# A spectral mixing layer and an MLP on one core: the sum of two loaded pieces made by an accumulating DMA instead of by VectorE

## The chip, the cores and the metric

The kernel runs on one core of one Trainium2 chip. The time is that of one execution on the device in microseconds, taken as the median of several runs. Beside it stands one execution recorded by the hardware profiler, whose span reaches from the first to the last instruction.

## What is computed

The input x has 2048 rows of 640 numbers, in float32. The reference normalizes each row, and adds three things: x itself, an MLP of the normalized rows with a GELU between two dense layers (640 to 1536 to 640), and a Fourier mixing of the normalized rows, of which only the real part is kept:

```python
xn = _layernorm(x)
a = einsum("bsd,ed->bse", xn, dft_hid_re)
b = einsum("bsd,ed->bse", xn, dft_hid_im)
y = einsum("ts,bse->bte", dft_seq_re, a) - einsum("ts,bse->bte", dft_seq_im, b)
out = x + y + gelu(xn @ w1 + b1) @ w2 + b2
```

Here `dft_seq_re` and `dft_seq_im` are 2048 x 2048 matrices that are inputs like any other; the kernel calls them cr and ci. The change lies in the stage that multiplies with these two (the sequence transform).

## The kernel before, in words

**Precision.** Every float32 operand of a product is kept as two parts of type float32r: ScalarE copies the high part (`high`, L186), VectorE subtracts it from the operand to get the low part (`low`, L189), and a product is three matmuls, high by high, high by low and low by high (`product`, L300 to L302). The two parts of a moving operand of the sequence transform lie in the tile `as`, which has three places that are used in turn.

**Blocks and pieces.** After the normalization, the MLP and the preparation of the stationary operands (the first 330 us) the sequence transform runs over 8 blocks (h, t): h is a half of the work along the sequence, t one of four groups of 512 rows of cr and ci. The order is h = 0 with t = 0 to 3, then h = 1 with t = 3, 0, 1, 2; after the sixth and the eighth block comes a stage that multiplies with the hidden-dimension matrices (`hidden_beside`, `hidden_entry`). For each block four raw pieces are loaded from DRAM: cr1, cr2, ci1 and ci2, the two halves of the columns of cr and of ci. A piece is 1 MB, and `steps_of_load` brings it in four DMAs of 256 KB, one for each quadrant of 32 partitions, in runs of 512 bytes, all issued by SyncE (L503). The pieces lie in the places `raw_a`, `raw_b` and, in the first half only, `raw_c`. `turn` (L520) then transposes a piece in 32 x 32 blocks on VectorE, in two halves u = 0, 1 (L524), out of `raw` into the tile where it is held: `r` for cr1 and cr2, `rt` for ci1 and ci2. When the second half of a piece has been transposed, its place is free, and `turn` issues the load of the piece that takes it next (`heir`). Two pieces of the last block are an exception: their loads are put off into the hidden stage before it (`put_off`, L1616 and L1618).

**Seven products.** A block takes seven products instead of eight, in the manner of Strassen, which need sums of the pieces. VectorE makes them in place on the held tiles, each in two halves: f5 puts ci1 + ci2 on ci1 (L563), f6 adds that to cr1, f3 adds the new cr1 to cr2, and f7 subtracts ci2 from cr1; all go through `add` (L463). The products use, in this order, cr1, cr2, ci1 (the sum), cr1 after f6, cr2 after f3, cr1 after f7, and ci2. ci1 as loaded is used for nothing but f5.

**The order of the work.** It is written out by hand, and every engine runs its own instructions in that order. A block is 14 entries (seven products by two halves u) of 18 matmuls each in the first three products and 12 in the others, with 12 more in entry 12. Entry n does its matmuls, then the steps in `pre`, then `form(n + 3)`, which makes the two parts for the third entry after it, then the steps in `post`. `beside` (L1328) gives `pre` and `post`: in the first block the transposition of ci2 and f5, f6, f3, f7; in the others f6, f3 and f7 of the block itself, the transpositions of the next block's pieces (ci1 beside entries 2 and 3), the sums that collect the results, and their loads and stores. f5 for a later block stands behind the last entry of the block before (L1436, L1473) or beside the first entries of the hidden stage (L1589, L1590). In the first block the transposition of ci1 comes ahead of the loop: behind it VectorE makes the last stationary operands (`build`, part "c") and then the low part for entry 3.

**Queues.** SyncE issues nearly all DMAs. GpSimd issues the stores of intermediate results in the first 266 us and a few stores of the output at the end.

Of the kernel before, what the change touches and what calls it, by code (L numbers as in the profile page):

```python
# [13 lines left out]
ALU = mybir.AluOpType  # L14

P = 128
Q = 4
B = 32
# [8 lines left out]
def kernel(  # L27
# [45 lines left out]
    nc = tc.nc  # L73
# [388 lines left out]
    def add(dst, a, b, op=ALU.add):  # L462
        nc.vector.tensor_tensor(dst, a, b, op=op)  # L463
# [28 lines left out]
    def steps_of_load(g):  # L492
        if g is None:
            return []
        h, t, kind = pieces[g]
        m, half = KINDS[kind]
        r = A["raw3"] if home[g] == "c" else A["raw"]
        raw[g] = r.tile([P, NB, NK * B], F32, tag=f"raw_{home[g]}", bufs=1, name=f"raw{g}")
        v = rows_of((cr, ci)[m], t)

        def quadrant(q):
            s0 = q * SQ + (half * NS // 2 + h * NK) * B
            nc.sync.dma_start(raw[g][q * B : (q + 1) * B], v[:, :, s0 : s0 + NK * B])  # L503

        return [lambda q=q: quadrant(q) for q in range(Q)]

    def held(kind, u):

        return {
            "cr1": lambda: A["r01"][:, 0, u],  # L510
            "cr2": lambda: A["r01"][:, 1, u],
            "ci1": lambda: A["rt2"][:, 0, u],
            "ci2": lambda: A["rt2"][:, 1, u],
        }[kind]()
# [32 lines left out]
    def form(n):  # L547
# [7 lines left out]
        else:  # L555
# [3 lines left out]
                split(a[:, 0], a[:, 1], src)  # L559
            else:  # L560
                split(a[:, 0, 0], a[:, 1, 0], src)

    def f5(u):  # L563
        add(held("ci1", u), held("ci1", u), held("ci2", u))

    def f6(u):
        add(held("cr1", u), held("cr1", u), held("ci1", u))
# [760 lines left out]
    def beside(h, t, n):  # L1328
# [14 lines left out]
        def g(k, acc, first=False, op=ALU.add):  # L1343
            return lambda: gather(h, t, k, acc, first, op)
# [18 lines left out]
        if b == 0:  # L1363
            T = lambda k, u: (lambda: turn(piece[0, 0, k], u))
            pre = {
                11: [g("v2", x_)],
            }.get(n, [])
            post = {
                0: [T("ci2", 0), F(f5, 0)],
                1: [g("u1", x_, True), T("ci2", 1), F(f5, 1), F(f6, 0), F(f6, 1)],  # L1370
                2: [lambda: load_xo(NT - 1)],
                3: [F(f3, 0), g("u", us, True)],
                4: [F(f3, 1), g("u1", y_)],
                5: [g("v2", z_, True), F(f7, 0)],
                6: [F(f7, 1)],
                7: [g("u2", x_, True), nturn("ci1", 0)],
                8: [nturn("ci1", 1)],
                9: [nturn("cr1", 0)],
                10: [g("u2", z_)],
                11: [nturn("cr1", 1)],  # L1380
                12: [nturn("cr2", 0)],
                13: [nturn("cr2", 1), nturn("ci2", 0), nturn("ci2", 1)],
            }.get(n, [])
        else:
            pre = {
                0: [F(f3, 0)] if ahead else [F(f6, 0)],
                1: [F(f3, 1)] if ahead else [F(f3, 0)],
                2: [nturn("ci1", 0)],
                3: [nturn("ci1", 1)],
                4: [F(f7, 0)],  # L1390
                5: [F(f7, 1)],
                6: [nturn("cr2", 0)],
                7: [nturn("cr2", 1)],
                8: [nturn("cr1", 0)],
                9: [nturn("cr1", 1)],
                10: [g("u2", z_)],
                11: [g("v2", x_)],
                12: [nturn("ci2", 1)] if direct else [nturn("ci2", 0)],
            }.get(n, [])
            post = {  # L1400
                0: [] if ahead else [F(f6, 1)],
                1: [g("u1", x_, True)] + ([] if ahead else [F(f3, 1)]),
                3: [g("u1", y_), g("u", us, True)],
                4: [t1(0)] if second else [],
                5: [g("v2", z_, True)],
                6: [t1(2)] if second else [],
                7: [g("u2", x_, True)],
                11: [nturn("ci2", 0)] if direct else [],
                12: [] if direct else [nturn("ci2", 1)],
                13: [t1(1)] if second else [],  # L1410
            }.get(n, [])
        if h == 0:
# [19 lines left out]
                }.get(n, [])  # L1432
            elif n == 13:
                post.append(lambda: later.append(lambda: put(h, t, "v", "v1")))
            if n == 13:
                post += [lambda: f5(0), lambda: f5(1)]  # L1436
        else:
            if p == 0 and n in (9, 10):
                post.append(lambda: load_part(blocks[b + 1][1], ("u1", "u")[n - 9]))
# [30 lines left out]
            if n == 13 and p == 1:  # L1470
                post += [lambda: open_g(b), lambda: [load_g(b, i) for i in range(3, len(A["g", b]))]]
            if n == 13 and direct:
                post += [g("v", vs, op=ALU.subtract), g("v1", x_), lambda: f5(0), lambda: f5(1)]  # L1473
        return pre, post


# [33 lines left out]
    def hidden_beside(b, n):  # L1510
# [64 lines left out]
        def last_columns():  # L1575
# [3 lines left out]

        yb1, yb2 = in_two(0), in_two(1)  # L1580
        yb4 = to(yo[tb, 4], vs, f"yb4_{tb}", lambda: store(tb, yo[tb, 4], 4 * B, DQ, *((nc.gpsimd,) if last else ())))
        f5s = [lambda u=u: f5(u) for u in range(2)] if not last else [lambda: None] * 2
        f6s = [lambda u=u: f6(u) for u in range(2)] if not last else [lambda: None] * 2
        v1 = lambda: add(s(1, "v1"), s(1, "v1"), x_)
        end = lambda: add(bank(X + 1), bank(X + 1), A["end"])
        pre = [v1] if n == 17 and not last else []
        post = {

            0: [lambda: gather(1, tb, "v1", z_), lambda: gather(1, tb, "v", vs, op=ALU.subtract), f5s[0]],  # L1589
            1: [f5s[1]],  # L1590
            3: [to(ya[:, :, : 2 * B], x_, f"ya1_{ta}")],
            2: [last_columns] if last else [],
            4: [t2(0)],
# [163 lines left out]
```

## Time and profile before

| | |
|---|---|
| median of 3 runs | 852.09 us (851.99 to 852.13) |
| profiled execution: span | 849.9 us |
| median of the runs less that span (what lies around it) | 2.2 us |
| instructions | 10599 |
| TensorE, VectorE, ScalarE, GpSimd busy | 841.9, 686.7, 368.6, 67.7 us |
| DMA moved | 166.53 MB, 196 GB/s on the mean |
| sequence transform with the hidden stages, first to last matmul | 330.30 to 844.57 us |

The profile names the engines PE (TensorE's matmuls), PEld (its loading of weights), DVE (VectorE), ACT (ScalarE), POOL (GpSimd) and SP (SyncE); a "q" behind a name marks the engine's own sequencer, which issues DMAs. L503 is line 503 of the kernel. `rt<-raw` means that tile rt is written from tile raw. A row of the groups gives line, engine, operation, tiles and shapes, the count behind "x", then busy time in us, the mean ns of one, the idle time before them and what ended it. A row of the timeline gives start and length in us, the engine, the line, the operation, the tiles, and in brackets how long the engine had been idle and what released it. A row of one line or tile gives the shortest, median and longest duration in ns and the first and last start in us, and for DMAs a line with the shortest, median and longest time from issue to landing. A row of the windows gives the stretch, its length, each engine's busy time and instructions in the order PE, PEld, DVE, ACT, POOL, then TensorE's granted clock, the share of the 16 DMA engines and GB/s. A row of the waits gives who waited for whom, the total in us, how often, and the longest.

### The profile page before, as it was taken

The numbers are of one execution on the slowest core, as the hardware profiler recorded it, in microseconds if no ns is written. First come the engines' busy times: TensorE is split into PE (matmuls) and PEld (weight loads), VectorE is DVE, ScalarE is ACT, GpSimd is POOL, SyncE is SP. The second block draws the span as 40 slices with busy tenths as digits, with TensorE's granted clock in tenths as the row PEclk, the third lists the DMA queues.
The fourth block names the chain that finished last, engine by engine and source line by source line (L and its number), as shares of the span: only waits on it lengthen the run. The fifth ranks groups of instructions, "written<-read, shape, count | busy, mean of one in ns | idle before, by whom it ended". The sixth has DMA issues, their size and how long they took to land.

```text
span 849.9 us, 10599 instructions
## 1 busy us (share of the span) xinstructions
PE 841.9 (99%) x3711; PEld 696.7 (82%) x3711; DVE 686.7 (81%) x909; ACT 368.6 (43%) x527; POOL 67.7 (8%) x116
## 2 busy tenths in 40 slices
PE   8999999999999999999999999999999999999997
PEld 7888888888888888888888888888888888888886
DVE  7979889767844778979978887889967998885687
ACT  7655666654453555443444344232323433323241
POOL 0440024222301000000000000000000000000002
PEclk9999999999999999999999999999999999999999
DMA  8995667878977897958744679763745799705464
GB/s 230 288 248 158 139 163 250 260 223 305 262 192 199 333 323 138 209 120 193 158 137 107 167 220 283 165 144 99 214 150 156 229 237 234 303 19 180 124 172 108
DMA packets 199141, 166.53 MB, mean 196 GB/s; under 512 B 61648, under 2 KB 170192, under 8 KB 198576
## 3 DMA queue, kind: packets, MB, share of 16 engines
q1 hardware_dynamic: 188320, 140.42, 62.7%
q0 software_dynamic: 7600, 24.91, 8.7%
q10 hardware_dynamic: 3168, 0.52, 0.3%
q8 instruction: 29, 0.48, 0.2%
q14 instruction: 24, 0.20, 0.1%
HBM read 115.75 MB, written 46.14 MB: 190 GB/s over the span
## 4 chain that ended last, share of the span: by engine, by line
PE 98%; DMA 1%; DVE 0%; ACT 0%; SPq 0%; issue 0%; ACTq 0%
PE banks L301 29%; PE banks L302 29%; PE banks L300 29%; PE banks L320 10%; DMA row<-in_A_x_dram 1%; PE banks L682 0%; DVE st L215 0%; ACT xp L714 0%; SPq L208 0%; DVE yo L1722 0%; DVE mv L216 0%; ACT mv L707 0%; DVE mv L708 0%; ACTq L707 0%
## 5 line engine op out<-in xcount | busy, mean ns | idle before, releaser
L186 ACT ACTIVATE as<-r 128x1024 fp32r<-128x1024 f32 x80 | 85.0, 1062 | 171.1 <-PE banks L302 150.4
L300 PE MATMUL banks<-as,xab 128*128 128x512 f32 x407 | 158.3, 389 | 0.0
L302 PE MATMUL banks<-as,xab 128*128 128x512 f32 x407 | 158.3, 389 | 0.0
L301 PE MATMUL banks<-as,xab 128*128 128x512 f32 x407 | 158.3, 389 | 0.0
L189 DVE TENSOR_TENSOR as<-r,as 128x1024 fp32r<-128x1024 f32 x80 | 97.2, 1215 | 38.1 <-ACT as L186 38.0
L301 PEld LDWEIGHTS banks<-as,xab 128*128 128x128 f32 x407 | 76.4, 188 | 15.9
L302 PEld LDWEIGHTS banks<-as,xab 128*128 128x128 f32 x407 | 76.4, 188 | 15.8
L300 PEld LDWEIGHTS banks<-as,xab 128*128 128x128 f32 x407 | 76.4, 188 | 15.8
L300 PE MATMUL banks<-as,xc 128*128 128x512 f32 x224 | 87.1, 389 | 0.0
L301 PE MATMUL banks<-as,xc 128*128 128x512 f32 x224 | 87.1, 389 | 0.0
L302 PE MATMUL banks<-as,xc 128*128 128x512 f32 x224 | 87.1, 389 | 0.0
L186 ACT ACTIVATE as<-rt 128x1024 fp32r<-128x1024 f32 x32 | 34.0, 1063 | 72.5 <-PE banks L302 57.9
L320 PE MATMUL banks<-xt,xab 128*128 128x512 f32 x240 | 56.8, 390 | 0.0
L189 DVE TENSOR_TENSOR hs<-ab,hs 128x512 fp32r<-128x512 f32 x36 | 24.7, 685 | 37.6 <-ACT hs L186 37.6
L320 PEld LDWEIGHTS banks<-xt,xab 128*128 128x128 f32 x240 | 45.0, 188 | 9.4
L301 PEld LDWEIGHTS banks<-as,xc 128*128 128x128 f32 x224 | 42.1, 188 | 8.8
L302 PEld LDWEIGHTS banks<-as,xc 128*128 128x128 f32 x224 | 42.0, 188 | 8.7
L300 PEld LDWEIGHTS banks<-as,xc 128*128 128x128 f32 x224 | 42.1, 188 | 8.7
L1280 POOL DMA_DIRECT2D out_dram<-u x4 | 2.6, 658 | 568.8 <-DVE u L463 568.8
L302 PE MATMUL banks<-hs,xc 128*128 128x512 f32 x120 | 46.7, 389 | 0.0
L300 PE MATMUL banks<-hs,xc 128*128 128x512 f32 x120 | 46.7, 389 | 0.0
L301 PE MATMUL banks<-hs,xc 128*128 128x512 f32 x120 | 46.7, 389 | 0.0
(240 smaller groups left out, 1678.9 us busy)
## 6 DMA issues: line engine op xcount, KB each, us to landing
raw<-in_A_dft_seq_re_dram SPq DMA_DIRECT2D x64, 256.0 KB, 5.4
raw<-in_A_dft_seq_im_dram SPq DMA_DIRECT2D x64, 256.0 KB, 5.1
w1r<-in_B_w_dram SPq DMA_DIRECT2D x144, 80.0 KB, 3.5
wit<-wst POOLq DMA_DIRECT2D x15, 384.0 KB, 4.2
wit<-wst POOLq DMA_DIRECT2D x20, 256.0 KB, 4.5
forms_ab<-xab SPq DMA_DIRECT2D x4, 1280.0 KB, 7.7
xab<-wit SPq DMA_DIRECT2D x13, 384.0 KB, 4.5
row<-xn SPq DMA_DIRECT2D x14, 320.0 KB, 5.3
```

Of the source, the lines that this page charges most:

```text
L186: nc.scalar.activation(h, s, AF.Copy)
L189: nc.vector.tensor_tensor(l, s, h.bitcast(F32), op=ALU.subtract)
L300: nc.tensor.matmul(acc, wh, mh, start=first, stop=False, skip_group_check=goes_on)
L301: nc.tensor.matmul(acc, wh, ml, start=False, stop=False, skip_group_check=goes_on)
L302: nc.tensor.matmul(acc, wl, mh, start=False, stop=last, skip_group_check=goes_on)
L320: nc.tensor.matmul(acc, W1[i][:, a, j * P : (j + 1) * P], XT[j][:, b], start=n == 0, stop=n == len(steps) - 1)
L1280: queues[q % len(queues)].dma_start(rows_of(out, t)[:, :, q * DQ + c0 : q * DQ + c1], src[q * B : (q + 1) * B])
```

## The change

For a piece of kind ci1 `steps_of_load` gives eight steps in place of four: after the four loads of ci's first half by SyncE come four DMAs issued by GpSimd, which read the second half from DRAM and add it onto the same quadrants of the raw piece (`accum_op=ALU.add`). The transposition of ci1 then brings ci1 + ci2 into the held tile, and f5 goes, with all its calls. ci2 is still loaded and transposed as a piece of its own.

```diff
-        def quadrant(q):
+        def quadrant(q, half=half, eng=nc.sync, **how):
             s0 = q * SQ + (half * NS // 2 + h * NK) * B
-            nc.sync.dma_start(raw[g][q * B : (q + 1) * B], v[:, :, s0 : s0 + NK * B])
-
-        return [lambda q=q: quadrant(q) for q in range(Q)]
+            eng.dma_start(raw[g][q * B : (q + 1) * B], v[:, :, s0 : s0 + NK * B], **how)
+
+        steps = [lambda q=q: quadrant(q) for q in range(Q)]
+        if kind == "ci1":
+            steps += [lambda q=q: quadrant(q, 1, nc.gpsimd, accum_op=ALU.add) for q in range(Q)]
+        return steps
...
-    def f5(u):
-        add(held("ci1", u), held("ci1", u), held("ci2", u))
...
-                0: [T("ci2", 0), F(f5, 0)],
-                1: [g("u1", x_, True), T("ci2", 1), F(f5, 1), F(f6, 0), F(f6, 1)],
+                0: [T("ci2", 0)],
+                1: [g("u1", x_, True), T("ci2", 1), F(f6, 0), F(f6, 1)],
...
-            if n == 13:
-                post += [lambda: f5(0), lambda: f5(1)]
...
-                post += [g("v", vs, op=ALU.subtract), g("v1", x_), lambda: f5(0), lambda: f5(1)]
+                post += [g("v", vs, op=ALU.subtract), g("v1", x_)]
...
-        f5s = [lambda u=u: f5(u) for u in range(2)] if not last else [lambda: None] * 2
...
-            0: [lambda: gather(1, tb, "v1", z_), lambda: gather(1, tb, "v", vs, op=ALU.subtract), f5s[0]],
-            1: [f5s[1]],
+            0: [lambda: gather(1, tb, "v1", z_), lambda: gather(1, tb, "v", vs, op=ALU.subtract)],
```

## The prediction

> **What bounds the kernel now.** I read the page first, then the waits of TensorE alone, then the busy time of the sequence stage as one window.
>
> ```profile
> PE 841.9 (99%) x3711; PEld 696.7 (82%) x3711; DVE 686.7 (81%) x909; ACT 368.6 (43%) x527; POOL 67.7 (8%) x116
> ```
>
> ```profile
> PE banks L666 <- DVE warm L657: 1.9, 1, 1.9
> PE banks L682 <- ACT xp L714: 0.7, 1, 0.7
> ```
>
> ```profile
> 330.30:844.60 514.30, 514.27 (x2269) 425.63 (x2267) 433.88 (x403) 179.58 (x186) 5.16 (x8) 1.00 0.66 173
> ```
>
> TensorE is busy for 841.9 of 849.9 us. Its only two waits are in the start-up, and in the 514.30 us that hold all products with the sequence matrices it is idle for 0.03 us, at a granted clock of 1.00. One matmul takes 514.27 / 2269 = 0.2267 us there. So the bound is TensorE, and no work taken from VectorE can shorten this stage. What can change the time is a form (the `as` tile, two parts made by ScalarE and VectorE) that comes later than the matmuls that need it. I therefore asked for VectorE's timeline at each piece and compared the end of each subtraction with the start of its matmuls.
>
> **What the change removes.** f5 is a VectorE addition in place, twice in each of 8 blocks:
>
> ```profile
> L463 DVE TENSOR_TENSOR rt<-rt 128x1024 f32<-128x1024 f32 x16 | 19.0, 1216 | 0.1
> ```
>
> 16 x 1.216 = 19.5 us of VectorE go. They lie beside matmuls: TensorE never waits for VectorE in this stage, so their price now is 0, and their removal gains at most the 0.03 us of idle time above. No stall goes, so nothing is late next. The room that it gives VectorE (2.4 us in each block) counts only where VectorE must catch up.
>
> **What it adds.** 32 DMAs of 256 KB, issued by GpSimd, each adding a quadrant of the second half onto a quadrant that SyncE has just loaded, and each waiting for that load to land. The nearest rows for GpSimd's part are these:
>
> ```profile
> L1280 POOL DMA_DIRECT2D out_dram<-u x4: 648/656/672, 834.7 to 836.7; - x4
> ```
>
> ```profile
> L931 POOL DMA_DIRECT2D gs<-v x5: 542/547/568, 103.4 to 175.9; - x5
> DMA to landing us min/median/max: 2.4/3.5/4.6
> ```
>
> ```profile
> L1280 POOL DMA_DIRECT2D out_dram<-u x4 | 2.6, 658 | 568.8 <-DVE u L463 568.8
> ```
>
> The first has the same shape (32 partitions by 16 rows), so I take 0.66 us to issue one; 32 of them are 21 us on GpSimd, which has nothing else to do before 834.7 us (in the third row it has been idle for the 568.8 us before). Behind a waiting accumulation only the next ones are queued. The second row, plain 256 KB stores by GpSimd, gives the shortest time from issue to landing, 2.4 us: 0.54 us of issue, about 1.24 us of moving (next paragraph), and 0.6 us of tail.
>
> The wait moves to the transposition of ci1 (L524). VectorE works in order, so behind it stand every later subtraction, and TensorE behind those. The piece with the least room is the first one.
>
> ```profile
> L503 SPq DMA_DIRECT2D raw<-in_A_dft_seq_im_dram x4: 312/486/487, 325.6 to 327.0; - x4
> DMA to landing us min/median/max: 3.3/4.5/5.6
> ```
>
> ```profile
> 332.98 2.36 DVE L524 STREAM_TRANSPOSE rt<-raw 128x1024 f32<-128x1024 f32 x2
> 335.27 0.38 DVE L463 TENSOR_TENSOR sums<-xc,sums 128x256 f32<-128x256 f32 x1
> ...
> 338.65 1.23 DVE L189 TENSOR_TENSOR as<-r,as 128x1024 fp32r<-128x1024 f32 x1
> ...
> 341.06 1.22 DVE L463 TENSOR_TENSOR rt<-rt 128x1024 f32<-128x1024 f32 x1
> ...
> 349.32 1.22 DVE L189 TENSOR_TENSOR as<-rt,as 128x1024 fp32r<-128x1024 f32 x1
> ```
>
> ```profile
> 342.54 0.39 PE L300 MATMUL banks<-as,xab 128*128 128x512 f32 x1
> ```
>
> The four quadrants land from 325.6 + 3.3 = 328.9 to 327.0 + 5.6 = 332.6 us, 1.24 us apart, and the transposition follows at 332.98. After it VectorE works without a break worth naming (the last operands of the stationary side) until the subtraction for entry 3 ends at 338.65 + 1.23 = 339.88, 6.9 us after the transposition began. Entry 3 starts on TensorE at 342.54. If the sum lands at T, entry 3 can start at T + 6.9, so the stall is T + 6.9 - 342.54 = **T - 335.6**. The margin is 3.0 us after the landing of today's last quadrant. Once TensorE has stalled, it cannot make the time up. The tightest entry today is 5: its subtraction ends at 350.54 and its matmuls start 36 later, at 342.54 + 36 x 0.2267 = 350.70. With two additions gone (that at 341.06 is one) VectorE needs 2.4 us less from entry 3 to entry 5, so these two follow without a stall of their own.
>
> How late is T? The transfers are crowded there:
>
> ```profile
> 326.00:332.00 6.00, 6.00 (x28) 4.99 (x27) 5.69 (x6) 4.68 (x8) 0.00 (x0) 1.00 0.95 193
> 332.00:338.00 6.00, 6.00 (x28) 4.96 (x27) 4.95 (x10) 1.96 (x5) 0.00 (x0) 1.00 1.23 222
> 338.00:344.00 6.00, 6.00 (x28) 4.98 (x27) 4.63 (x5) 2.21 (x3) 0.00 (x0) 1.00 1.24 216
> ```
>
> The DMA share (last but one column) is 0.95 to 1.24: SyncE has twelve quadrants in flight, this piece's and the next two's. The first accumulation is issued when the first quadrant has landed and can move from 328.9 + 0.66 = 329.6 us; from then on each shares the engines with one of SyncE's quadrants (1.24 us). No row shows an accumulating transfer. Lower bound of its moving time: 1.24 us, that of a plain one; T = 329.6 + 4 x (1.24 + 1.24) + 0.6 = 340.1, stall 4.5 us. Double, because the old values must be read as well as the new: 2.48 us; T = 329.6 + 4 x 3.72 + 0.6 = 345.1, stall 9.5 us. The most favourable T, with no sharing at all, is 332.6 + 2.4 = 335.0: no stall. I take the middle of the two shared cases, 1.9 us, since nothing in the trace speaks for either: T = 342.8, **stall 7.1 us**. A row that points the same way is that of GpSimd's stores beside SyncE's loads at 262 us, on the same crowded engines:
>
> ```profile
> L956 POOL DMA_DIRECT2D ys<-xo x3: 1111/1219/1337, 262.5 to 264.6; - x3
> DMA to landing us min/median/max: 6.6/8.4/9.4
> ```
>
> With 6.6 to 9.4 us from issue to landing, T would be 332.6 + 6.6 to 9.4 = 339.2 to 342.0.
>
> [...]
>
> The last block has the next smallest room, because its load is put off to the hidden stage:
>
> ```profile
> L503 SPq DMA_DIRECT2D raw<-in_A_dft_seq_im_dram x4: 486/487/530, 686.8 to 688.4; - x4
> DMA to landing us min/median/max: 3.9/4.9/5.8
> ```
>
> ```profile
> 698.63 1.24 DVE L524 STREAM_TRANSPOSE rt<-raw 128x1024 f32<-128x1024 f32 x1
> ...
> 702.87 1.23 DVE L189 TENSOR_TENSOR as<-r,as 128x1024 fp32r<-128x1024 f32 x1 [0.62 <-ACT as L186]
> ...
> 711.03 1.23 DVE L189 TENSOR_TENSOR as<-r,as 128x1024 fp32r<-128x1024 f32 x1 [1.59 <-ACT as L186]
> ...
> 720.25 1.18 DVE L189 TENSOR_TENSOR as<-r,as 128x1024 fp32r<-128x1024 f32 x1
> ```
>
> ```profile
> 723.34 0.39 PE L300 MATMUL banks<-as,xc 128*128 128x512 f32 x1
> ```
>
> The quadrants land from 690.7 to 694.2; the transposition is at 698.63. The subtraction that ends at 721.43 has 1.9 us before its matmuls at 723.34, and VectorE's idle times before it (0.62 and 1.59 us) absorb 2.2 us more, so the sum may land up to 4.1 us late, at 702.7. By the same working T = 690.7 + 0.66 + 4 x (1.9 + 1.24) + 0.6 = 704.5 (SyncE's stores to the output run beside it): **stall 1.8 us**; 0 with 1.24 us, 4.1 with 2.48 us.
>
> The others have more room. The nearest two are these:
>
> ```profile
> L503 SPq DMA_DIRECT2D raw<-in_A_dft_seq_im_dram x4: 311/487/488, 375.5 to 376.9; - x4
> DMA to landing us min/median/max: 3.3/4.8/6.0
> ```
>
> ```profile
> 395.08 1.23 DVE L524 STREAM_TRANSPOSE rt<-raw 128x1024 f32<-128x1024 f32 x1
> ```
>
> ```profile
> L503 SPq DMA_DIRECT2D raw<-in_A_dft_seq_im_dram x4: 550/1034/3057, 514.1 to 517.2; - x4
> DMA to landing us min/median/max: 9.4/9.8/10.1
> ```
>
> ```profile
> 539.05 1.24 DVE L524 STREAM_TRANSPOSE rt<-raw 128x1024 f32<-128x1024 f32 x1
> ```
>
> Their first quadrants land at 378.8 and 523.5, so the sums land 13.8 us later, at 392.6 and 537.3, ahead of 395.08 and 539.05. The stall in the first block shifts all of these alike, since each load waits for a transposition. The remaining four have longer from issue to transposition than these and enter with nothing.
>
> **The sum.** 7.1 + 1.8 = 8.9 us on the profiled span. That execution has a span of 849.9 us; the median of the runs is 852.09 us, 2.2 us of it outside the span, which the change does not touch. 852.1 + 8.9 = **861.0 us**.
>
> **The rivals.**
> - Not slower: the accumulations move beside SyncE's loads without sharing, and the first sum lands by 335.6 us. It decides at L524 of the first block, and its price is 0: 852.1 us. For it: the shortest GpSimd row, 2.4 us, would do. Against it: the engines are full there, and the same row's median, 3.5 us, gives T = 336.1, already late. Chance 0.12.
> - Much slower: an accumulation is handled row by row, with its reads and writes not overlapped, say four times a plain quadrant (4.96 us). Then a sum lands 0.66 + 4 x 6.2 + 0.6 = 26.1 us after the first quadrant: first block at 355.0, a stall of 19.4 us; last at 716.8, 14.1 us; the two at 395.08 and 539.05 are 9.8 and 10.6 us late at 404.9 and 549.6, part of which VectorE's idle times absorb. That is 885.6 to 906 us; with a factor of three (21.1 us after the first quadrant) the first and last blocks give 14.4 + 9.1 us, 875.6 us, and those two up to 10 us more. For it: only that no row shows such a transfer. Chance 0.2, half of it beyond 878.
> - Faster: VectorE's 19.5 us would have to be on the path. The idle 0.03 us speaks against it: at best 852.0. Chance 0.02, for chance effects.
> - The forecast, stalls in the first and perhaps the last block, 856.6 (1.24 us) to 865.7 us (2.48 us): chance 0.66.
>
> **How the numbers follow.** The predicted time is the forecast's. The range, 853.0 to 878.0 us, reaches down to a first sum at about 336.5 us and up to a factor of three; it leaves out most of the first rival and half of the second, about 0.2. About 0.2% (1.7 us) is what a measurement of this kernel can tell from no change: slower by more than that 0.86, within it 0.12, faster 0.02.
>
> **What would show it.** In the profile of the changed kernel: TensorE idle a few us once, near 342 us, waiting for the subtraction of entry 3; VectorE idle before L524 there until a DMA onto `raw` has landed; perhaps a second, smaller gap near 705 to 725 us; none near 395 and 540; the subtractions and transpositions as long as now; 32 issues of about 0.66 us on GpSimd. The prediction is wrong if TensorE shows no gap (an accumulation costs no more than 2.4 us in the crowd), if gaps stand in most blocks (it costs three times a load or more), or if SyncE's loads themselves are so late that VectorE waits for pieces other than ci1.

## The result, and the profile after

The changed kernel takes 870.02 us (median of 4 runs, 868.47 to 872.83) against 852.04 us for the kernel before beside it on the same chip (851.51 to 852.13): a ratio of 1.0216, interval 1.0204 to 1.0228. It is 18.0 us slower. The sign and the range of the prediction held; the size did not: 8.9 us were forecast. The profiled execution takes 870.94 us with a span of 869.0 us. Its page, in the lines that answer to those of before:

```profile
PE 845.2 (97%) x3711; PEld 698.2 (80%) x3711; DVE 669.8 (77%) x893; ACT 368.1 (42%) x527; POOL 102.2 (12%) x148
PEclk9999999999999999799999999999999999999999
L503 POOL DMA_DIRECT2D raw<-in_A_dft_seq_im_dram x32 | 34.4, 1245 | 409.0 <-DMA raw<-in_A_dft_seq_im_dram 310.9
L527 DVE STREAM_TRANSPOSE rt<-raw 128x1024 f32<-128x1024 f32 x32 | 38.8, 1230 | 24.4 <-DMA raw<-in_A_dft_seq_im_dram 24.3
```

VectorE lost 16 additions and 16.9 us of work, and the kernel lost 18 us. The last row says where to look: VectorE stood idle for 24.3 us ahead of the transposition of ci1 (L524 before, L527 now) until a DMA had landed. The 7 in the row of the granted clock is new as well. TensorE's waits, all others being in the start-up (total, count, longest):

```profile
PE banks L300 <- ACT as L186: 10.7, 1, 10.7
PE banks L301 <- DVE as L189: 3.2, 2, 2.8
```

Three waits, in two places, where the prediction expected one and perhaps a second gap. First TensorE's and VectorE's timelines in the first block:

```profile
342.96 0.39 PE L302 MATMUL banks<-as,xab 128*128 128x512 f32 x1
354.04 0.79 PE L300 MATMUL banks<-as,xab 128*128 128x512 f32 x1 [10.70 <-ACT as L186]
355.31 0.79 PE L301 MATMUL banks<-as,xab 128*128 128x512 f32 x1 [0.47 <-DVE as L189]
```

```profile
348.36 2.37 DVE L527 STREAM_TRANSPOSE rt<-raw 128x1024 f32<-128x1024 f32 x2 [14.65 <-DMA raw<-in_A_dft_seq_im_dram]
...
354.02 1.23 DVE L189 TENSOR_TENSOR as<-r,as 128x1024 fp32r<-128x1024 f32 x1
```

Entry 3 waits for its two parts, made by ScalarE and VectorE. VectorE's part ends at 354.02 + 1.23 = 355.25, 6.9 us after the transposition began at 348.36, exactly as long as worked out. So in the first block the chain from the landing of the sum, T, to TensorE is right. T is not: 348.3 us. Here are the four accumulations, and the twelve loads of SyncE around them (durations in ns, first and last start, then the time from issue to landing):

```profile
L503 POOL DMA_DIRECT2D raw<-in_A_dft_seq_im_dram x4: 1126/1730/2357, 333.8 to 335.8; - x4
DMA to landing us min/median/max: 7.8/11.2/12.4
```

```profile
L503 SPq DMA_DIRECT2D raw<-in_A_dft_seq_im_dram x12: 311/488/1170, 326.3 to 335.3; - x12
DMA to landing us min/median/max: 3.1/5.7/10.6
```

The first quadrant lands at 326.3 + 3.1 = 329.4 us, and the accumulations at 341.6, 345.2, 346.8 and 348.3. Between 329.4 and 348.3 the trace shows eleven more quadrants of SyncE's landing: three of ci1, four of ci2, four of the second block's ci1.

Then the clock. The windows behind the gap (last but two column: TensorE's granted clock):

```profile
343.00:354.00 11.00, 0.34 (x2) 0.00 (x0) 4.80 (x8) 2.00 (x4) 2.12 (x2) 0.70 1.39 196
354.00:356.00 2.00, 1.49 (x3) 0.89 (x4) 1.98 (x2) 2.00 (x3) 0.00 (x0) 0.50 1.25 228
356.00:358.00 2.00, 2.00 (x7) 1.57 (x6) 2.00 (x3) 0.79 (x1) 0.00 (x0) 0.57 0.60 104
358.00:360.00 2.00, 2.00 (x11) 1.63 (x10) 2.00 (x3) 0.00 (x0) 0.00 (x0) 1.00 0.04 13
```

For 3.6 us after the gap the clock is half, and matmuls start 0.43 us apart in place of 0.227. From 342.96 to the ninth matmul behind it, at 358.11, pass 15.15 us where nine starts need 2.04: **the first block loses 13.1 us**, about 12.1 by waiting (entry 3 was due at 342.96 + 0.23 = 343.19, and its second part is there at 355.25) and 1.0 by the clock.

```profile
358.11 0.39 PE L302 MATMUL banks<-as,xab 128*128 128x512 f32 x1
```

The last block's sum, with VectorE's and TensorE's timelines and a window behind the gap:

```profile
720.20 1.25 DVE L527 STREAM_TRANSPOSE rt<-raw 128x1024 f32<-128x1024 f32 x1 [7.70 <-DMA raw<-in_A_dft_seq_im_dram]
```

```profile
721.37 1.18 DVE L189 TENSOR_TENSOR as<-rt,as 128x1024 fp32r<-128x1024 f32 x1
```

```profile
719.44 0.39 PE L300 MATMUL banks<-as,xab 128*128 128x512 f32 x1
722.61 0.54 PE L301 MATMUL banks<-as,xab 128*128 128x512 f32 x1 [2.78 <-DVE as L189]
...
726.36 0.40 PE L301 MATMUL banks<-as,xab 128*128 128x512 f32 x1
```

```profile
723.00:725.00 2.00, 2.00 (x6) 1.60 (x5) 2.00 (x3) 0.00 (x0) 0.00 (x0) 0.50 1.19 228
```

This wait stands among the matmuls of the seventh block, beside whose entries 2 and 3 VectorE transposes the last block's ci1. TensorE waits for the second part of entry 5 there (L189 at 721.37), which does not use the late sum: its operand is the seventh block's own, of which ScalarE made the first part at 711.48 us. It only stands behind the transposition in VectorE's order. The last block's sum is first used at 761.03 us, 41 us after it landed:

```profile
711.48 1.06 ACT L186 ACTIVATE as<-rt 128x1024 fp32r<-128x1024 f32 x1 [3.02 <-PE banks L302]
...
761.03 1.06 ACT L186 ACTIVATE as<-rt 128x1024 fp32r<-128x1024 f32 x1 [3.01 <-PE banks L302]
```

By the same count, from 719.44 to the tenth matmul behind it at 726.36 (6.92 us where ten starts need 2.27), **the last block's sum costs 4.7 us**: 2.9 by waiting (722.61 less 719.67, when the matmul was due), 1.7 by the clock (rounded). Where the text says that the last block loses or waits, it means this place. 13.1 + 4.7 = 17.8 us of the 18.0. The span of this execution is 19.1 us longer; the other 1.3 us lie in the start-up and the tail, and its own time is 0.9 us above the median.

### The profile page after: what moved, and what is told of

The parts are those of the page before. It is cut to its first block, busy times and chain, and to the rows that moved or that the text cites. A ratio compares the mean times of both kernels' runs of the same rounds, so it can differ in the third digit from the quotient of the medians.

```text
span 869.0 us, 10681 instructions
## 1 busy us (share of the span) xinstructions
PE 845.2 (97%) x3711; PEld 698.2 (80%) x3711; DVE 669.8 (77%) x893; ACT 368.1 (42%) x527; POOL 102.2 (12%) x148
## 4 chain that ended last, share of the span: by engine, by line
PE 91%; DMA 4%; DVE 2%; ACT 1%; issue 1%; SPq 1%; POOL 0%; DVEq 0%; ACTq 0%
PE banks L301 27%; PE banks L302 27%; PE banks L300 27%; PE banks L320 9%; DMA raw<-in_A_dft_seq_im_dram 4%; DVE rt L527 0%; DVE r L527 0%; PE banks L666 0%; POOL raw L503 0%; SPq L1280 0%; DVE as L189 0%; PE banks L682 0%; DMA w1r<-in_B_w_dram 0%; ACT ob L1293 0%; ACT as L186 0%
## 5 line engine op out<-in xcount | busy, mean ns | idle before, releaser
L300 PE MATMUL banks<-as,xab 128*128 128x512 f32 x407 | 159.7, 392 | 10.7 <-ACT as L186 10.7
L189 DVE TENSOR_TENSOR as<-r,as 128x1024 fp32r<-128x1024 f32 x80 | 97.3, 1217 | 44.3 <-ACT as L186 44.2
L503 POOL DMA_DIRECT2D raw<-in_A_dft_seq_im_dram x32 | 34.4, 1245 | 409.0 <-DMA raw<-in_A_dft_seq_im_dram 310.9
L527 DVE STREAM_TRANSPOSE rt<-raw 128x1024 f32<-128x1024 f32 x32 | 38.8, 1230 | 24.4 <-DMA raw<-in_A_dft_seq_im_dram 24.3
L189 DVE TENSOR_TENSOR hs<-ab,hs 128x512 fp32r<-128x512 f32 x36 | 24.7, 686 | 38.3 <-ACT hs L186 38.3
L302 PE MATMUL banks<-hs,xc 128*128 128x512 f32 x120 | 46.7, 389 | 0.0
L300 PE MATMUL banks<-hs,xc 128*128 128x512 f32 x120 | 46.7, 389 | 0.0
```

What stands on the lines that cost most here:

```text
L189: nc.vector.tensor_tensor(l, s, h.bitcast(F32), op=ALU.subtract)
L300: nc.tensor.matmul(acc, wh, mh, start=first, stop=False, skip_group_check=goes_on)
L302: nc.tensor.matmul(acc, wl, mh, start=False, stop=last, skip_group_check=goes_on)
L503: eng.dma_start(raw[g][q * B : (q + 1) * B], v[:, :, s0 : s0 + NK * B], **how)
L527: nc.vector.transpose(held(pieces[g][2], u).rearrange("p c (n i) -> p c n i", i=B), r.rearrange("p n (c i) -> p c n i", i=B))
```

## The experiments

The theory, from the trace: the whole loss is two sums that land too late, and they are late because the accumulations stand in line behind the loads of SyncE that are already under way. The rivals: the loss lies elsewhere; an accumulation is slow in itself; GpSimd starts late. The kernel before was timed beside each: 851.4 to 852.0 us.

### Where the loss is: e1_middle, e2_first, e3_last, e10_none

```diff
-        if kind == "ci1":
+        if kind == "ci1" and g // Q in SUMMED:
...
+        if k not in SUMMED:
+            add(held("ci1", u), held("ci1", u), held("ci2", u))
```

SUMMED is (1, ..., 6), (0,) and (7,) in the first three; in the other blocks f5 is VectorE's addition, where it was. The fourth has `if False:` there and no f5.

> Accumulation in blocks 1 to 6 only; the first and the last block add on VectorE as before. Theory (all the loss lies in two waits of VectorE, in the first and the last block): no gap of TensorE after the start-up, 852 us, ratio 1.000 within 0.002. Rival (the 8 MB more of transfers and the work on GpSimd slow every block): about three quarters of the loss stays, 864 us or more.

> Accumulation in the first block only. Theory: the stall of about 12 us near 343 us stays, with about 1 us more of slow matmuls after it; no gap near 720 us: about 865 us. Rival (the stall comes from the next piece's accumulations and loads on the same queues): the sum lands several us earlier, since no accumulation of the second block's piece follows, and the time is below 860 us.

> Accumulation in the last block only. Theory without a first-use delay: a gap of about 3 us near 706 us and 2 us of slow matmuls after it, about 857 us. If GpSimd's first accumulating DMA starts about 3.5 us late wherever it stands (as the first block's did: 4.07 us from its last wait to its start, 0.5 us for the others), that delay is found here too, the gap is about 6 to 7 us and the time about 860 us.

> The changed kernel without the 32 accumulations: f5 is gone and nothing stands in its place, so the products that should use ci1 + ci2 use ci1 alone. What the removal of VectorE's 19.5 us gains by itself. The prediction's step says nothing: 851.5 to 852.3 us, the ratio within 0.1% of one. The rival, that part of the 18 us is lost by the changed order or the changed program and not by the accumulations, or that the removal gains and hides a still larger loss: over 853 or under 851 us.

| | time, us | ratio, interval |
|---|---|---|
| e1_middle | 852.14 | 1.0006, 0.9997 to 1.0015 |
| e2_first | 866.02 | 1.0172, 1.0155 to 1.0189 |
| e3_last | 863.61 | 1.0141, 1.0126 to 1.0156 |
| e10_none | 851.73 | 1.0003, 0.9994 to 1.0012 |

TensorE's longest wait of e2_first, then of e3_last:

```profile
PE banks L300 <- ACT as L186: 11.0, 1, 11.0
```

```profile
PE banks L301 <- DVE as L189: 9.0, 1, 9.0
```

24 accumulations in the six middle blocks cost nothing, and all 16 additions taken away gain nothing: both steps of the prediction hold. e2_first loses 14.4 us, about what the first block loses in the changed kernel (13.1), though no other accumulation stands behind it. e3_last lost 12 us, more than the last block loses in the changed kernel (4.7) and more than both forecasts (857 and 860 us in place of 863.61). The trace gives a hint: its first accumulation starts 5.3 us after its last wait was over, as it does 4.1 us late in the first block of the changed kernel and 4.8 us late in e2_first; in e1_middle it takes 0.6 us. This late start was the next question.

### GpSimd's late start: e4_warm, e11_pad

```diff
+    nc.gpsimd.memset(padl, 0.0)
...
     load_a(0)
+    nc.gpsimd.dma_start(padl[:B], x[:B, :PADL], accum_op=ALU.add)
```

e11_pad has the same line without `accum_op`.

> As the change, with one tiny accumulating DMA (32 rows of 8 numbers onto a tile that nothing reads) issued by GpSimd at about 265 us. If the first one of its kind costs 3.5 us more to start, the first block's sum lands about 3.5 us earlier and the stall falls from 12 to about 8.5 us: about 866.5 us against 870. Rival (the late start has another cause, such as the wait for all four loads): no change, 870 us.

> As the kernel with a tiny accumulating transfer on GpSimd at 266 us, but that transfer is a plain one. It tells apart what removed the 3.5 us by which GpSimd's first accumulation had started late. If the place in GpSimd's program decides (the block of its instructions that is fetched at about 331.5 us in both), the plain transfer shifts it as the accumulating one did: the first accumulation starts 0.5 us after its last wait, near 330.3 us. If the first accumulating transfer of a program is slow to start, it starts 4 to 5 us after its wait, near 333.8 us. The time is 869 to 870.5 us either way, since the last landing moved by 1.0 to 1.3 us only.

Times: 869.96 us (ratio 1.0216, 1.0200 to 1.0231) and 869.56 us (1.0213, 1.0195 to 1.0232). GpSimd's timelines of e4_warm, then of e11_pad:

```profile
330.27 4.38 POOL L503 DMA_DIRECT2D raw<-in_A_dft_seq_im_dram  x4 [62.73 <-DMA raw<-in_A_dft_seq_im_dram]
```

```profile
330.91 4.42 POOL L503 DMA_DIRECT2D raw<-in_A_dft_seq_im_dram  x4 [62.04 <-ACT ob L1295]
```

One small transfer more in GpSimd's program, plain or accumulating, takes the late start away (0.5 us from the wait to the start in both). So it does not belong to the first accumulating transfer; in e5_plain below, where GpSimd's transfers do not add, the first one starts 4.5 us late too. What is left is the place of the instruction in GpSimd's program, which these runs suggest and do not prove. In the late cases a block of 8192 bytes on the queue that the page calls "q14 instruction" moves within the delay (331.55 us in the changed kernel, 331.23 in e2_first, 694.53 in e3_last); in e4_warm one moves at the same time without a delay of that size, so the fetch as its cause is only argued. For the time it hardly mattered in the first block: the start came 3.5 and 2.9 us earlier and the sum landed at 346.95 and 348.12 us, so e4_warm's forecast of 866.5 us failed. Something else sets T.

### The line or the add: e5_plain, e7_quiet, e8_alone

e5_plain takes `accum_op=ALU.add` off the 32 transfers. e7_quiet:

```diff
-    load_a(4)
...
     turn(2, 0)
     turn(2, 1)
+    load_a(4)
```

e8_alone is e4_warm with that, and with ci2's load (`load_a(heir[1])`, which the second piece's `turn` issued) in the same place; ci2 is transposed beside entries 4 and 5.

> GpSimd's 32 transfers stay with their size, their waits and their order, but do not add: each writes the second half over the first, so the products that should use ci1 + ci2 use ci2 alone. The theory of the line (the DMA engines serve transfers in the order of their issue, and a transfer of GpSimd's waits for the five or six quadrants of SyncE's that were issued ahead of it, then takes 1.4 us itself): the first sum's last landing comes only 0.2 us earlier per transfer than the accumulating ones, at about 347 us in place of 348.3, TensorE's gap near 343 is 10 to 12 us, and the time is 867 to 870 us. The rival, that the add itself is the price (the old values are read as well as the new): a plain transfer lands 1.24 us behind the one before, the last one at 340 to 343 us, the gap is 4 to 7 us, and the time 857 to 864 us.

> All accumulations stay. The load of the second block's ci1 (four quadrants by SyncE, and its four accumulations), which was issued at 331.8 us ahead of the first block's accumulations, is issued behind the transposition of the first block's sum. The theory of the line: with four quadrants of 1.24 us fewer ahead, the first accumulation lands at about 338.2 in place of 341.6 us, the others 1.4 to 1.5 us apart up to 342.6 to 343.5, the gap falls from 10.7 to 5 to 7 us, and the time to 864 to 866 us. The rival, that an accumulation takes 2.4 to 3.6 us of the engines by itself: the last landing stays at 346 to 349 us and the time at 868 to 871 us.

> As the kernel with the tiny accumulating transfer at 266 us (so that GpSimd's first accumulation starts half a microsecond after its wait), and besides the load of the first block's ci2 and that of the second block's ci1 are issued behind the transposition of the first block's sum, so that nothing but ci1's own quadrants lies ahead of its accumulations; the transpositions of ci2 stand ahead of f7. The theory of the line: the four accumulations land at about 334, 335.5, 336.9 and 338 us (4.4 us after an issue that follows each quadrant by 0.6 us), the gap is 1 to 3 us, and the time 858 to 861 us, what is left being the last block's loss of 4.8 us and the gap. The rival, accumulations slow by themselves: landings 2.4 to 3.6 us apart, the last at 342 to 345 us, a gap of 5 to 9 us, 863 to 868 us.

The accumulations of e7_quiet, then of e8_alone, and the plain transfers of e5_plain in the first block:

```profile
L503 POOL DMA_DIRECT2D raw<-in_A_dft_seq_im_dram x4: 1126/1730/2362, 333.6 to 335.6; - x4
DMA to landing us min/median/max: 4.8/6.6/8.0
```

```profile
L503 POOL DMA_DIRECT2D raw<-in_A_dft_seq_im_dram x4: 1109/1246/1500, 329.3 to 332.4; - x4
DMA to landing us min/median/max: 4.2/6.1/6.6
```

```profile
L503 POOL DMA_DIRECT2D raw<-in_A_dft_seq_im_dram x4: 648/656/672, 333.6 to 335.6; - x4
DMA to landing us min/median/max: 7.4/9.0/11.3
```

Without the add the last one still needs 11.3 us (12.4 with it). With four of SyncE's quadrants fewer on the way, the same accumulations, started at the same time, need 8.0 us. In the first block that is the line, not the add. With the runs below, the landing of the sum against SyncE's quadrants that land after ci1's first one and before the sum:

| | first quadrant lands | SyncE's quadrants in between | sum lands | difference |
|---|---|---|---|---|
| changed kernel | 329.4 | 11 | 348.3 | 18.9 |
| e2_first | 328.3 | 11 | 347.4 | 19.2 |
| e6_later | 328.6 | 11 | 348.2 | 19.6 |
| e11_pad | 329.7 | 10 | 348.1 | 18.4 |
| e4_warm | 329.1 | 9 | 346.9 | 17.9 |
| e7_quiet | 328.6 | 7 | 343.6 | 15.0 |
| e13_order | 328.0 | 7 | 342.0 | 14.0 |
| e8_alone | 328.1 | 3 | 339.0 | 10.9 |
| e12_room | 329.1 | 3 | 339.7 | 10.6 |

From 3 to 11 quadrants the difference grows by (18.9 - 10.75) / 8 = 1.02 us for each, and what is left for the four accumulations is 7.7 us. The other rows lie up to 1.0 us off that line. A sum that lands late for another reason would also let more quadrants pass, so the count alone proves nothing; two edits do, since they change which loads SyncE has on the way: e7_quiet takes away four of the changed kernel's quadrants and 3.9 us, e8_alone six of e4_warm's and 7.0 us. In the first block the number of quadrants ahead sets T, and the late start adds little.

The times: e5_plain 865.23 us (1.0157, 1.0140 to 1.0174), e7_quiet 867.00 us (1.0181, 1.0166 to 1.0196), e8_alone 862.61 us (1.0124, 1.0109 to 1.0139). e7_quiet and e8_alone are 1.0 and 1.6 us above the upper ends of their forecasts, though the landings are as expected within 1 us: the forecasts left too little for the half clock. In e8_alone the first block loses 5.7 us: two waits of 3.5 us together, where 1 to 3 were forecast, and the rest behind them, with 3.4 us at half the clock. e5_plain lies between the times of the two theories, 857 to 864 and 867 to 870, and tells something that neither had: its gap in the first block is 9.9 us, as the theory of the line said, but in the last block TensorE does not wait at all. There the add does cost. The accumulations of the changed kernel in the last block, and the plain ones of e5_plain:

```profile
L503 POOL DMA_DIRECT2D raw<-in_A_dft_seq_im_dram x4: 1062/1289/1559, 705.3 to 708.7; - x4
DMA to landing us min/median/max: 7.6/10.6/11.4
```

```profile
L503 POOL DMA_DIRECT2D raw<-in_A_dft_seq_im_dram x4: 648/650/657, 704.5 to 707.6; - x4
DMA to landing us min/median/max: 6.4/7.1/7.8
```

Beside SyncE's stores of the output the slowest accumulating transfer takes 3.6 us longer to land than the slowest plain one, in the first block beside its loads 1.1 us. In the seven kernels that accumulate in the first and the last block as the changed one does, the last block's sum lands 14.1 to 16.1 us after its first quadrant, in e5_plain 11.7 us after it. Why the two places differ was not settled.

The line stands in the last block too. There eight of SyncE's transfers land between the first quadrant (704.3 us) and the sum (720.1): three quadrants and five stores of the output, 2112 KB in all. In e3_last, whose accumulations start later, it is sixteen transfers with 3840 KB, and the sum lands 22.0 us after the first quadrant in place of 15.8: 6.3 us for the bytes of 6.75 quadrants, 0.93 us for each. So there the late start seems to have cost time by what it let go ahead.

### The clock behind a gap: e9_filler

```diff
                 sequence_entry(n, what, w, u)
+                if n == 2:
+                    for _ in range(46):
+                        nc.tensor.matmul(
+                            bank(Z), A["xab", 0][:, 0, :P], A["as"][:, 2, 0, 0], start=True, stop=True
+                        )
```

> The changed kernel, with 46 more matmuls (10.4 us at 0.227 us) behind entry 2 of the first block, into a bank that is free there; their results are used for nothing. They fill the time in which TensorE waits for the first sum. The theory that the half granted clock behind a stall comes from the idle time: the granted clock stays at 1.00 from 343 to 360 us, the matmuls of entry 3 are 0.23 us apart from the first one, the loss there falls by 1.0 us and the time to about 869 us. The rival, that the clock drops for another reason (the transfers, or the operands' arrival): the matmuls behind 354 us are 0.43 us apart all the same, and the time stays at 870 us. Where the sum lands does not change in either.

```profile
341.00:352.00 11.00, 11.00 (x51) 9.09 (x50) 3.56 (x6) 0.36 (x2) 2.91 (x3) 1.00 1.43 187
352.00:354.00 2.00, 1.35 (x6) 0.72 (x4) 1.58 (x3) 2.00 (x4) 0.00 (x0) 1.00 1.21 250
354.00:356.00 2.00, 1.24 (x5) 0.86 (x5) 2.00 (x3) 2.00 (x3) 0.00 (x0) 1.00 1.20 232
```

The windows of e9_filler show a granted clock of 1.00 throughout, where the changed kernel has 0.50 from 347.5 to 357.7 us, with the sum landing as late as before (347.9 us). So it is the idle time here that makes the clock drop, and 10 us of useless matmuls make the kernel faster: 867.21 us (1.0185, 1.0170 to 1.0201). That is 15.8 us above the kernel before that was timed beside it, in place of 18.0: 2.2 us less, more than the 1.0 us forecast; in this run the gap in the last block is also smaller, 1.1 us, and no half clock follows it. Half the clock was granted for 3.6 us behind the 10.7 us gap of the changed kernel, and for 6.8 us in e6_later, in stretches of 3.4 us (see the end); a gap of 2.8 us had it too (the last block of the changed kernel).

### Whether the loss can be had back: e6_later, e12_room, e13_order, e14_both, e15_two

e6_later, in the first block:

```diff
-    turn(2, 0)
-    turn(2, 1)
     build(len(builds) - 1, "c")
...
-                0: [T("ci2", 0)],
-                1: [g("u1", x_, True), T("ci2", 1), F(f6, 0), F(f6, 1)],
-                2: [lambda: load_xo(NT - 1)],
+                0: [T("ci1", 0)],
+                1: [g("u1", x_, True), T("ci1", 1)],
+                2: [F(f6, 0), F(f6, 1), T("ci2", 0), T("ci2", 1), lambda: load_xo(NT - 1)],
```

> All accumulations stay. In the first block only, the two transpositions of the sum are moved behind the last operands of the stationary side and the low part of entry 3, and those of ci2 behind them. VectorE then does not hold back entry 3, and the first entry that needs the sum is entry 4, which starts about 4.1 us after entry 3. If the stall is the landing of the first sum at 348.3 us and VectorE's order behind it, the gap near 343 goes, one of 3.4 to 5 us comes near 347 to 352 us, before the low part of entry 4, and the time falls by 6 to 8 us, to 862 to 864 us. If the loss had another place (transfers later in the stage, or VectorE's own work), the time stays at 869 to 871 us.

862.78 us (1.0132, 1.0117 to 1.0148). TensorE's first wait:

```profile
PE banks L300 <- ACT as L186: 4.3, 1, 4.3
```

As forecast. The sum lands when it did (348.2 us) and a gap stands only ahead of entry 4, which needs the sum itself. Part of the first block's stall was VectorE's order: entry 3 does not use ci1, and stood behind its transposition. e12_room puts this, the extra transfer and the two loads held back together, and leaves the last block to f5.

> Accumulations in the first seven blocks; in the last block f5 stays on VectorE and there is no accumulation. In the first block three of the edits of the runs before stand together: the tiny accumulating transfer at 266 us, the loads of ci2 and of the second block's ci1 behind the transposition of the sum, and that transposition behind the low part of entry 3 (ci2's ahead of f7). If the loss is the landing of two sums against the entry that needs them and nothing else: the first sum lands at about 339 us, entry 4 needs its low part at 347 us, no gap, and the time is 851.7 to 853 us, that of the kernel before. If a loss belongs to the accumulations themselves (contention with VectorE's or TensorE's accesses, which 28 of them would show): 855 us or more.

863.82 us (1.0148, 1.0131 to 1.0165): the forecast of 851.7 to 853 failed. TensorE's only wait behind the start-up, and the accumulations of the second block's ci1:

```profile
PE banks L301 <- DVE as L189: 9.0, 1, 9.0
```

```profile
L503 POOL DMA_DIRECT2D raw<-in_A_dft_seq_im_dram x4: 1058/1062/1077, 358.3 to 361.8; - x4
DMA to landing us min/median/max: 9.3/11.4/13.6
```

The first block's own sum lands at 339.7 us, and nothing waits for it. The wait begins at 369.0 us, near the end of the first block, beside whose entries 7 and 8 the second block's ci1 is transposed: this ci1, held back, is loaded behind ci2, its accumulations start at 358.3 and end at 361.8 + 13.6 = 375.5 us, and VectorE waits for them. The edit had moved the late sum one block on. So the next one holds back ci2 only:

```diff
-                1: [g("u1", x_, True), T("ci1", 1), lambda: load_a(heir[1]), lambda: load_a(4)],
+                1: [g("u1", x_, True), T("ci1", 1), lambda: load_a(heir[1])],
```

with `load_a(4)` where it was, and ci2's transpositions beside entries 5 and 6. e14_both adds the last block's accumulations with their load four entries earlier (`if n == 14: post.append(lambda: load_a(put_off[0]))` in place of 18), e15_two two entries earlier (16).

> As e12_room (accumulations in the first seven blocks, the tiny accumulating transfer at 266 us, the first block's transposition of the sum behind the low part of entry 3), but of SyncE's loads only that of the first block's ci2 is held back; the second block's ci1 is loaded when it was, and ci2 is transposed beside entries 5 and 6, ahead of f7. The theory of the line: four quadrants of SyncE's lie ahead of the first accumulation or between them, the first sum lands at 343 to 345 us, entry 4 (needed from 347 us on) waits 0 to 1 us, the second block's sum lands before 360 us and nobody waits for it; 851.5 to 853.5 us. The rival, that the first seven accumulated sums cost time by themselves: 855 us or more with gaps at other places.

> All 32 accumulations, with the first block as in e13_order, and in the stage before the last block the load of ci1 (with its accumulations) four entries earlier, behind entry 14 in place of entry 18. The theory: the last sum then lands some 12 to 16 us earlier, ahead of its transposition, and both losses are gone: 851.5 to 853.5 us, the time of the kernel before, since TensorE bounds both. The rival, that the last block loses time to transfers and not to the landing of the sum (SyncE's stores of the output were slower beside the accumulations): gaps stay near 710 to 730 us and the time is 855 us or more. No theory expects less than the kernel before.

> As e14_both, with the load of the last block's ci1 two entries earlier than in the changed kernel (behind entry 16) in place of four, so that it stands behind the loads of the hidden stage's matrices (the last of them was issued at 672.5 us). The theory that only the late landing of the two sums costs time: the waits for gr and gr_b near 680 us are gone, the sum lands by 700 us and nobody waits for it, 852 to 854.5 us, with the small waits of e13_order (about 1 us near 365 and 374 us) as the rest. The rival, that the accumulations in the stage before the last block cost 2 to 4 us wherever they are put: 855.5 us or more.

| | accumulations | time, us | ratio, interval |
|---|---|---|---|
| e13_order | blocks 1 to 7 | 853.26 | 1.0025, 1.0015 to 1.0034 |
| e14_both | all 32 | 857.85 | 1.0068, 1.0048 to 1.0087 |
| e15_two | all 32 | 854.18 | 1.0031, 1.0020 to 1.0043 |

TensorE's waits of e15_two, all of them, and the longest of e14_both:

```profile
PE banks L667 <- DVE warm L658: 1.9, 1, 1.9
PE banks L683 <- ACT xp L715: 1.1, 1, 1.1
PE banks L300 <- DVE v L463: 0.8, 1, 0.8
PE banks L300 <- ACT u L1269: 0.6, 1, 0.6
```

```profile
PE banks L300 <- DMA gr_b<-wit: 2.6, 1, 2.6
```

e14_both missed its forecast of 851.5 to 853.5 us: the load that was moved up stood ahead of the last loads of the hidden stage's matrices in SyncE's queue, and TensorE waited for those. Two entries later that is gone. With all 32 accumulations in place, 15.8 of the 18 us are back, and no wait on a sum is left. The two small waits behind the start-up look like the price of ci2's load, held back; the chain that ended last in e13_order leads there:

```profile
351.18 7.45 DMA raw<-in_A_dft_seq_im_dram
358.65 1.25 DVE rt L527
...
373.62 1.14 DVE v L463
```

ci2 lands at 358.63, and the chain runs through VectorE from its transposition to the end of TensorE's wait at 374.81 us. No version is faster than the kernel before, and none can be by much: that one has TensorE idle for 0.03 us in this stage.

## Where the prediction was right, and why its size was wrong

- **What bounds the kernel**: right. VectorE's 19.5 us gained nothing (e10_none, 1.0003).
- **Where it stalls**: right. The first and the last block, once each, no other (e1_middle).
- **From the landing to TensorE**: right in the first block. T + 6.9 us is when entry 3 can start.
- **The landing in the first block: the step that failed.** It said "from then on each shares the engines with one of SyncE's quadrants", four in all, and took 1.9 us for the moving of an accumulation, so T came 13.9 us after the first quadrant. The runs show 18.9 us, with eleven quadrants of SyncE's in between, 1.02 us for each, and 7.7 us for the four accumulations. With four quadrants that would be 7.7 + 4 x 1.02 = 11.8 us: the price of an accumulation was taken too high, not too low; the seven quadrants left out are 7 x 1.02 = 7.1 us. That the too high price made up 2.1 us of them was luck. The prediction had "twelve quadrants in flight" a few lines earlier, and did not count them. The stall was mis-sized by that: 12.1 us against 7.1.
- **The last block**: T came 15.8 us after the first quadrant, 2.0 us later than worked out, and the stall is 2.9 us against 1.8. Here too eight of SyncE's transfers landed in between where four were counted, and the add itself costs (e5_plain). The wait is also another one than the prediction named: not ahead of the matmul that stood at 723.34 us in the kernel before, but at the one that stood at 705.89, in entry 5 of the seventh block.
- **The clock**: no term of the sum. A stall was priced by its length; 1.0 and 1.7 us more went to the half clock behind it (e9_filler).
- **The issue**: 0.66 us was expected, as for a plain transfer. One alone takes 1.06 us (the row of e12_room above), in a row up to 2.4. GpSimd had the time, so it cost nothing by itself.
- **The doubled case** (2.48 us for an accumulation, a first stall of 9.5 us): an assumption of the prediction that no run shows. That the measured 12.1 us lie nearer to it than to the 7.1 forecast does not speak for it. Plain transfers in the first block are late as well (11.3 us to the landing of the slowest in e5_plain, against 12.4 with the add), and four accumulations alone do not take twice as long as four quadrants: behind the first block's, where none of SyncE's transfers lay between them, they landed at 348.28, 349.75, 351.23, 352.66 and 354.18 us, 1.5 us apart, against 1.2 for SyncE's.

5.0 us of the missing 9.1 are the first block's landing, 2.7 the clock, 1.1 the last block's landing; the 0.3 that are left are less than the spread of the runs.

## What to carry to other kernels

In this kernel's first block a sum whose transfers are made to wait for others landed 1.02 us later for each of SyncE's quadrants that landed ahead of it (eleven in the changed kernel): count every transfer that is issued before it and not yet landed, not only those that run at its side. When a stall is priced, the engine's clock behind it belongs to the price (here 1.0 and 1.7 us), and when a load is moved to make room, the question is whose place in the queue it takes. Work moved from an engine off the critical path gained nothing here (e10_none, a ratio of 1.0003), and its new place, between a load and the transposition of what it loaded, was on the path twice (13.1 and 4.7 us). A step that waits for late data is better put behind the work that does not need them: e6_later did this for the first block's transposition. For the last block's sum, first used 41 us after it landed, it was not tried.

## What the runs showed of the hardware

- **Landings in the order of issue, in e13_order.** There SyncE's quadrants issued up to 328.93 us land at 331.70, 332.83, 334.09, 335.48 and 336.91, and GpSimd's accumulations, the first issued at 329.21, behind all of them, at 337.75 to 341.96; in e12_room one issued alike with nothing ahead but ci1 lands 4.5 us after its issue, here after 8.5. It is no fixed order: in the last block of the changed kernel a store of SyncE's issued at 704.18 us lands at 715.49, behind an accumulation issued at 705.34 that lands at 712.98. What decides was not found out.
- **A late start on GpSimd** of 4.1 to 5.3 us, which one more transfer before it removes (0.5 us in e4_warm and e11_pad).
- **The half clock came in stretches of 3.4 us.** In e8_alone the granted clock is half from 346.9 to 350.3 us, in e6_later from 351.0 to 357.8, in the changed kernel from 347.5 to 357.7: 3.4, 6.8 and 10.2 us, one, two and three times the first; in the last block of the changed kernel it is half from 722.9 to 726.3, 3.4 us again. It was seen behind gaps from 2.6 us up (e11_pad's in the last block), though not behind the 2.6 us of e14_both.
